# Two output tiles of batch 0 by seven half-size products, earlier loads, and VectorE's work in pairs of pairs

## The chip, the cores and the metric

The kernel runs on one core of a Trainium2 chip. A core has TensorE (PE in the profile; its weight loads are listed as PEld), VectorE (DVE), ScalarE (ACT), GpSimd (POOL) and SyncE (SP), each with its own instruction stream, and 16 DMA engines that all queues share. The engines run side by side and wait for one another through semaphores. The metric is the device time of one execution in microseconds (us), as the median of several runs.

## The reference

Two stages, in float32. The first is a block-sparse attention for 4 batches, 8 heads, 768 tokens and a head dimension of 64. Each query sees the 31 keys nearest to it and 24 block summaries (the maximum of 32 keys, the mean of 32 values); both share one softmax:

```python
k_sum = k.reshape(B, H, nb, block, D).max(axis=3)
v_sum = v.reshape(B, H, nb, block, D).mean(axis=3)
scores_l = scale * np.matmul(q, k.transpose(0, 1, 3, 2))      # masked to |i - j| < 16
scores_s = scale * np.einsum('bhsd,bhnd->bhsn', q, k_sum) + np.log(block)
a = softmax(np.concatenate([scores_l_masked, scores_s], axis=-1))
attn = np.matmul(a, np.concatenate([v, v_sum], axis=2))
```

The second is a feed-forward layer on the 3072 rows of 512 that come out of it (2048 hidden units):

```python
h = x @ w_in
g = h * (1.0 / (1.0 + np.exp(-1.702 * h)))
out = g @ w_out
```

## The kernel before, in words

Tokens are columns for most of the way. A batch has 768 tokens, split into two halves of 384 (`half` 0 and 1), each three tiles of 128. Heads go in four pairs (`p`), and two pairs make a group (`g`).

For each batch, the attention is: `scores` (small matmuls of keys with queries, then ScalarE's exponential into `a_sb`), `mask` (VectorE multiplies by `mk`), `values` (matmuls with the value rows `vw`, then VectorE's `norm`: a reciprocal and a multiplication for each pair, into `x2`), and a transposition into `xTT`: `tx` does it on TensorE with a copy by VectorE, `dx` by a DMA transpose of SP's queue. Keys stand in `kxs[s]` with three kinds of rows: their own, 16-column halos (`key_halos`) and the block maxima (`key_rows`); `rest_k` makes the maxima by a reduction and then the copies, for one pair. For batch 1 keys and queries are turned by TensorE (`tk`, `tq`), and there `rest_k` has its copies done by GpSimd; for batches 2 and 3 by DMA transposes (`xk`, `xq`). `value_rows` copies the values' halos by DMA, sums blocks of values on TensorE (`vsum`), adds them on VectorE (`block_sums`, into `vpart` and `vs`) and spreads the sums by two more DMAs (`sum_dmas`).

The feed-forward layer has a first matrix (`ff_in`, `ff_one`, `ff_open`: four matmuls of 384 columns for each of the 16 hidden tiles, then a gelu on ScalarE into `gTb`) and a second one in two forms. `ff_out` is the plain one: for an output tile of 128 tokens sixteen matmuls of 512 columns into one PSUM bank, in four parts. `product` is the other: the 2 x 2 blocks of two token tiles, hidden halves and output halves are multiplied with seven block products instead of eight, each of eight matmuls of 256 columns. That needs sums of weight blocks (`w_sum`, into `ws`) and of gelu tiles (`g_sums`, into `gs`), both on VectorE, and additions of the results on the way out (`keep_it`, `give`). The left tile of such a pair is tile t of half 0, the right one tile t of half 1.

Order: instructions stand on each engine's queue in the order of the program (`_Ordered`), so the order is written by hand. Batch 0's attention and half 0 come first (to line 1089). Then half 1 of batch 0 runs its first matrix (lines 1095 to 1099) with the `todo` list beside it: batch 1's turned keys and queries, and the sums of the weights. Its three output tiles follow, all plain (lines 1102 to 1108), with batch 1's attention beside them step by step (`plan1`, called by `beside`). The loop from line 1112 then takes batches 1 and 2: first matrix, then the three pairs of tiles by seven products in the order `seq`, with the next batch's attention beside them (`plan`). Batch 3 is done apart, with products in both matrices.

Loads: q, k and v come through GpSimd's queue, which also converts them (`load_turned`, `load_v`). A batch's loads are issued by `load_batch`: keys, values and queries. Two tiny GpSimd copies (`gate2`) hold the queue until certain transposes have landed, since they read what those write: lines 244 and 247 ahead of batch 3's keys and values, line 1133 ahead of batch 3's queries. At most eight loads of this queue are in flight; the next one waits for the one eight places before it.

PSUM banks for results come from two pools, `pmm` (tag `mm`, four banks) and `psb` (tag `big`, two double banks); a new tile waits until the readers of the bank's last contents are done.

Of the kernel before, what the change touches and what calls it, by code (L numbers as in the profile page):

```python
# [9 lines left out]
F32 = mybir.dt.float32  # L10
# [25 lines left out]
def kernel(  # L36
# [205 lines left out]
    def load_batch(b):  # L242
        if b == 3:
            pool.tensor_copy(out=gate2, in_=qTs[0][:, 0, 0:1])
        load_turned(k, b, kb2, "kb")
        if b == 3:
            pool.tensor_copy(out=gate2, in_=qTs[0][:, NP - 1, 0:1])
        if b == 1:
            load_turned(q, b, qb2, "qb", (0,))
        load_v(b)  # L250
        if b < 3:
            load_turned(q, b, qb2, "qb", (1,) if b == 1 else (0, 1))
# [89 lines left out]
    def flat_kx(p, s):  # L342
        return kx[p][s].rearrange("p t c -> p (t c)")

# [228 lines left out]

    def rest_k(p, s, eng=dve):
        ks = attp.tile([128, nb], BF16, name="ks", tag="ks")
        dve.tensor_reduce(out=ks.rearrange("p (j e n) -> p j e n", e=2, n=2),
                          in_=at(flat_kx(p, s), 0, [[256, NJ], [192, 2], [block, 2], [1, block]]),
                          axis=AX.X, op=ALU.max)
        key_halos(p, s, eng)
        key_rows(p, s, ks, eng)  # L580
# [16 lines left out]
    def values(b, half, g):  # L597
# [81 lines left out]
    def g_sums(j, eng=dve, which=(0, 1, 2, 3)):  # L679

        a1, a2 = gTb[:, j], gTb[:, j + NT // 2]
        l, r = slice(0, HALF), slice(HALF, S)
        for w in which:
            a, b_, op = {0: (a1[:, r], a2[:, r], ALU.add), 1: (gs[:, 0, j], a1[:, l], ALU.subtract),
                         2: (a1[:, l], a1[:, r], ALU.subtract), 3: (a2[:, l], gs[:, 1, j], ALU.subtract)}[w]
            eng.tensor_tensor(out=gs[:, w, j], in0=a, in1=b_, op=op)
# [84 lines left out]
    def product(b, t, what):  # L771
        n = NT // 2
        l = slice(t * 128, t * 128 + 128)
        r = slice(HALF + t * 128, HALF + t * 128 + 128)
        lo, hi = slice(0, N1), slice(N1, d_model)
        raw_l, raw_r = gTb[:, :, l], gTb[:, :, r]
# [41 lines left out]
        if what == 1:  # L818
            keep_it("s1")
        elif what == 2:  # L820
            give("o1", lo, "s1")
        elif what == 6:
            keep_it("s2")
        elif what == 5:
            keep_it("s5")
        elif what == 7:
            give("o2", hi, "s5")
            if last:
                store("o2", HALF + t * 128, hi)
        elif what == 3:  # L830
            give("o1", hi, "s2")
            store("o1", t * 128)
        else:
            give("o2", lo, None)
            store("o2", HALF + t * 128, lo if last else slice(0, d_model))
# [37 lines left out]
    gate2 = consts.tile([128, 1], BF16, name="gate2")  # L873
# [137 lines left out]
    for p in range(NP):  # L1011
# [5 lines left out]
    load_batch(1)  # L1017
# [6 lines left out]
             9: ["x00", "x01", "v10"], 10: ["v11"], 11: ["x10"]}  # L1024
# [59 lines left out]
    for i, (ms, part) in enumerate((ms, part) for part in range(4) for ms in range(JH)):  # L1084
        ff_out(0, ms, part)
        beside0(i)
        if i in (10, 11):
# [4 lines left out]
            6: [lambda: w_sum(2, 1)], 7: [lambda: w_sum(3, 0)], 8: [lambda: tk(2, 1, act)],   # L1092
            10: [lambda: w_sum(3, 1)], 9: [lambda: tq(0, 1, dve)], 11: [lambda: tk(3, 1, act)], 12: [lambda: tq(1, 1, dve)],
            15: [lambda: value_rows(1)]}
    ff_in(1, range(3))
    for nt in range(3, NT):
        ff_in(1, (nt,))
        for f in todo.get(nt, ()):
            f()
    exp_soon()  # L1100
    beside(1, -1)
    for i, (ms, part) in enumerate((ms, part) for ms in range(JH) for part in range(4)):
        ff_out(1, ms, part)
        beside(1, i)
        if i == 2:
            load_batch(2)
        if i in (9, 11):
            xk(i // 2 - 4, 0)
# [3 lines left out]
    for b in range(1, B - 1):  # L1112
# [5 lines left out]
        for n in range(0, NT, 2):  # L1118
            if n == 0:
                ff_open(order2[0:4], (lambda: tx(1, 1)) if b == 1 else None)  # L1120
            elif n == 2:
                for nt in order2[0:4]:
                    ff_one(1, nt)
                g_sums(0)
                g_sums(1)
            else:
# [3 lines left out]
                g_sums(n // 2, dve, (0, 1) if n + 2 == NT else (0, 1, 2, 3))  # L1130
# [15 lines left out]
        for t, what in seq:  # L1146
# [97 lines left out]
```

## Time and profile before

| what | value |
|---|---|
| median of three runs | 206.86 us (206.62 to 208.16) |
| the profiled execution | 206.51 us, of which 204.8 us is the span from the first to the last instruction |
| TensorE clock granted | 0.998 of full speed |
| instructions | 5857, of them 2364 matmuls |
| busy: TensorE, VectorE, ScalarE, GpSimd | 198.1, 140.4, 124.6, 92.7 us |
| HBM read, written | 27.26 MB, 6.29 MB |

Busy time is a mean over stages with different limits. The stages of this kernel in the span, by TensorE's chain: batch 0's attention to about 20 us; its first half's layer and second half's attention to 45; its second half's first matrix to 58; its second half's output with batch 1's attention to 75; batch 1's layer with batch 2's attention to 119.5; batch 2's layer with batch 3's attention to 163.5; batch 3's layer to the end. The profile's rows name what an instruction writes and reads, `out<-in`; a row of a group has the count, the sum of busy time, the mean of one in ns, the idle time of the engine before it and what ended that. In the timeline the first two numbers are start and duration in us.

### The profile page before, as it was taken

To read this page: it belongs to the slowest core of one execution; us is meant where nothing else is said; L and a number is where in the kernel's file an instruction comes from. 1 tells how busy PE (TensorE), PEld (TensorE's weight loads), DVE (VectorE), ACT (ScalarE), POOL (GpSimd) and SP (SyncE) were. 2 spreads that over 40 slices of the span, in tenths; PEclk is the share of its full clock that TensorE was granted. 3 is DMA by queue.
4 is the path that set the end of the run, shared out by engine and by line. 5 is a ranking of instruction groups with operands and counts; after the bars stand their busy time and mean duration, and the time that the engine had idled before them with its cause. 6 is when DMAs were issued, how large, how long until landed. Compare 5 with 4: busy or idle time off the path is not lost.

```text
span 204.8 us, 5857 instructions
## 1 busy us (share of the span) xinstructions
PE 198.1 (97%) x2364; PEld 137.4 (67%) x2364; DVE 140.4 (69%) x388; ACT 124.6 (61%) x238; POOL 92.7 (45%) x144
## 2 busy tenths in 40 slices
PE   6989999999999999999999999999999999999992
PEld 6667654556754566665888975657888865578881
DVE  6767894594856874897768689896759546658211
ACT  4385876638786717777871546778661467983220
POOL 7965389555999584002965035000000019990000
PEclk9999999999999999999999999999999999999999
DMA  5999999999999999999999989996023730000222
GB/s 117 153 159 202 207 211 213 195 156 232 134 143 151 177 176 168 159 175 132 123 196 127 154 151 142 122 261 137 0 106 90 160 111 3 0 0 3 102 102 104
DMA packets 95851, 27.93 MB, mean 136 GB/s; under 512 B 83649, under 2 KB 92881, under 8 KB 95825
## 3 DMA queue, kind: packets, MB, share of 16 engines
q0 software_dynamic: 69920, 13.44, 85.2%
q1 hardware_dynamic: 25904, 14.13, 33.2%
q8 instruction: 18, 0.29, 0.6%
q14 instruction: 9, 0.07, 0.1%
HBM read 27.26 MB, written 6.29 MB: 164 GB/s over the span
## 4 chain that ended last, share of the span: by engine, by line
PE 90%; DMA 4%; POOL 2%; DVE 1%; issue 1%; ACT 0%; POOLq 0%; DVEq 0%
PE ph L28 33%; PE poA L28 16%; PE po L28 11%; PE poB L28 7%; PE ps_av L28 4%; DMA v0n<-in_v_dram 4%; PE poC L28 4%; PE phA L28 4%; PE ps_s L28 3%; PE ps_t L28 1%; PE ps_x L28 1%; POOL kb L28 1%; PE phB L28 1%; PE phC L28 1%; PE phE L28 1%; PE ps_vs L28 1%
## 5 line engine op out<-in xcount | busy, mean ns | idle before, releaser
L28 PE MATMUL ph<-xT,w_in_sb 128*128 128x384 f16 x416 | 70.2, 326 | 0.1
L28 PEld LDWEIGHTS <-w_in_sb 128*128 128x128 f16 x452 | 43.7, 98 | 27.8 <-issue 0.2
L28 ACT ACTIVATE gT<-ph 128x384 f16<-128x384 f32 x104 | 49.9, 492 | 18.5 <-PE ph L28 18.1
L28 PEld LDWEIGHTS <-gT 128*128 128x128 f16 x312 | 28.8, 98 | 11.3 <-issue 0.2
L28 ACT ACTIVATE a_sb<-ps_s 128x768 bf16<-128x768 f32 (+1 forms) x32 | 25.0, 826 | 12.5 <-PE ps_s L28 12.5
L28 POOL DMA_DIRECT2D vw<-in_v_dram x36 | 24.6, 700 | 12.4 <-DMA kb<-in_k_dram 4.8
L28 PEld LDWEIGHTS <-gs 128*128 128x128 f16 x288 | 27.7, 98 | 3.4
L28 POOL TENSOR_TENSOR gs<-gT 128x384 f16<-128x384 f16 x9 | 8.2, 911 | 42.3 <-ACT gT L28 42.3
L28 PE MATMUL po<-w_out_sb,gT 128*128 128x512 f16 x96 | 23.6, 380 | 0.0
L28 DVE TENSOR_TENSOR a_sb<-a_sb,mk 128x768 bf16<-128x768 bf16 x28 | 14.9, 554 | 6.5 <-ACT a_sb L28 5.9
L28 PE MATMUL poA<-ws,gs 128*128 128x256 f16 x144 | 18.7, 273 | 0.0
L28 DVE TENSOR_TENSOR x<-ps_av,rc 128x384 f16<-128x384 f32 x32 | 17.8, 558 | 1.1
L28 DVE TENSOR_TENSOR gs<-gT 128x384 f16<-128x384 f16 (+1 forms) x34 | 13.4, 394 | 7.2 <-ACT gT L28 6.9
L28 POOL DMA_DIRECT2D qb<-in_q_dram x16 | 15.1, 956 | 1.8 <-DMA w_in_sb<-in_moe_w_in_dram 1.1
L28 POOL DMA_DIRECT2D kb<-in_k_dram x15 | 14.5, 976 | 0.9 <-POOLq L1228 0.8
L28 PEld LDWEIGHTS <-kx 64*128 64x128 bf16 (+1 forms) x372 | 9.4, 95 | 6.8 <-issue 4.4
L28 DVE TENSOR_REDUCE ks<-kx 128x24 bf16<-128x768 bf16 x12 | 11.4, 949 | 3.4 <-ACT kx L28 3.2
L28 ACT ACT_TABLE_LOAD x10 | 12.8, 1283 | 1.0 <-PEq L1228 0.8
L28 ACT ACTIVATE osb<-poA 128x256 f32<-128x256 f32 x9 | 3.5, 384 | 16.0 <-PE poA L28 16.0
L28 ACT ACTIVATE s<-poA 128x256 f32<-128x256 f32 x11 | 4.2, 386 | 11.2 <-PE poA L28 11.2
L28 PEld LDWEIGHTS <-a_sb 128*64 128x64 bf16 (+2 forms) x400 | 7.8, 108 | 2.8 <-issue 1.3
L28 PE MATMUL poA<-ws,gT 128*128 128x256 f16 x72 | 9.3, 273 | 0.0
(117 smaller groups left out, 282.7 us busy)
## 6 DMA issues: line engine op xcount, KB each, us to landing
out_dram<-osb SPq DMA_DIRECT2D x23, 256.0 KB, 3.3
kb<-in_k_dram POOLq DMA_DIRECT2D x15, 192.0 KB, 7.1
qb<-in_q_dram POOLq DMA_DIRECT2D x12, 192.0 KB, 10.9
vw<-in_v_dram POOLq DMA_DIRECT2D x36, 64.0 KB, 5.7
w_out_sb<-in_moe_w_out_dram POOLq DMA_DIRECT2D x4, 512.0 KB, 13.0
w_in_sb<-in_moe_w_in_dram POOLq DMA_DIRECT2D x3, 512.0 KB, 12.9
vw<-vs SPq DMA_DIRECT2D x6, 198.0 KB, 6.1
v0n<-in_v_dram POOLq DMA_DIRECT2D x4, 192.0 KB, 8.1
```

Source lines behind the costliest of these rows:

```text
L28: r = f(*a, **kw)
```

## The change

Four things change together.

1. Batch 0's second half: tile 0 (tile 3 of the batch) stays plain, tiles 1 and 2 are the left and right tile of one set of seven products. `product` takes the pair of tiles as an argument, and `g_sums_tiles` makes the sums for these two tiles alone, for two pairs of hidden tiles at once. The first matrix of this half runs its hidden tiles in the order j, j + 8 (`order2`) so that the sums can start early. The stretch has eleven steps where it had twelve, and `x10` moves up beside `v11`.
2. Batch 1's key rows: `rest_k` leaves `tk`, and with it GpSimd; `rest_k2` makes two pairs at once on VectorE, at steps 7 and 13 of the first matrix. Batches 2 and 3 use it too, two calls in place of four.
3. `g_sums` takes two hidden pairs at once where it can (n=2), and `values` norms both pairs of a group by one reciprocal and one multiplication for batches 2 and 3.
4. `load_batch` and the gates are gone. Batch 2's values are asked for ahead of batch 0's second first matrix, its keys at steps 7 and 12 of it, its queries at the third output step; batch 3's keys and queries during batch 1's first matrix, its values after batch 1's first product. The DMA transposes of keys move up to steps 4 and 7 of the output stage before, those of queries to the start of the next first matrix.

```diff
@@ new functions
+    def rest_k2(g, s):
+        flat = kxs[s].rearrange("p i t c -> p (i t c)")
+        o, n = 2 * g * NQ * 128, 2 * NJ
+        ks = attp.tile([128, 2, nb], BF16, name="ks", tag="ks")
+        dve.tensor_reduce(out=ks.rearrange("p i (j e n) -> p (i j) e n", e=2, n=2),
+                          in_=at(flat, o, [[256, n], [192, 2], [block, 2], [1, block]]),
+                          axis=AX.X, op=ALU.max)
+        dve.tensor_copy(out=at(flat, o + 256 + 96, [[256 * NJ, 2], [256, NJ - 1], [1, 16]]),
+                        in_=at(flat, o + 256 - 16, [[256 * NJ, 2], [256, NJ - 1], [1, 16]]))
...
+        for i in range(2):
+            key_rows(2 * g + i, s, ks[:, i])
+    def g_sums_tiles(j, L, R, eng):
+        js, js2 = slice(j, j + 2), slice(j + NT // 2, j + NT // 2 + 2)
+        l, r = slice(L * 128, L * 128 + 128), slice(R * 128, R * 128 + 128)
+        o = [gs[:, w, js, 0:128] for w in range(4)]
+        for w, (a, b_, op) in enumerate(((gTb[:, js, r], gTb[:, js2, r], ALU.add), (o[0], gTb[:, js, l], ALU.subtract),
+                                         (gTb[:, js, l], gTb[:, js, r], ALU.subtract),
+                                         (gTb[:, js2, l], o[1], ALU.subtract))):
+            eng.tensor_tensor(out=o[w], in0=a, in1=b_, op=op)
@@ tk
-        rest_k(p, s, pool)
@@ values
+        if b > 1:
+            pv = ps.rearrange("p (i c) -> p i c", i=2)[:, :, 0:390].rearrange("p i (n c) -> p i n c", c=D + 1)
+            rc = attp.tile([128, 2, 2 * JH, 1], F32, name="rc2", tag="rc2")
+            dve.reciprocal(out=rc, in_=pv[..., D:D + 1])
+            dve.tensor_mul(x2[g].rearrange("p h j i d -> p i (h j) d"), pv[..., 0:D],
+                           rc.to_broadcast([128, 2, 2 * JH, D]))
+            return
@@ plan1
-             9: ["x00", "x01", "v10"], 10: ["v11"], 11: ["x10"]}
+             9: ["x00", "x01", "v10"], 10: ["v11", "x10"]}
@@ batch 0, second half
-    ff_in(1, range(3))
-    for nt in range(3, NT):
-        ff_in(1, (nt,))
-        for f in todo.get(nt, ()):
+    load_v(2)
+    ff_in(1, order2[0:3])
+    for i in range(3, NT):
+        ff_in(1, (order2[i],))
+        for f in todo.get(i, ()):
             f()
+        if i in (6, 10, 14):
+            g_sums_tiles((i - 6) // 2, JH + 1, JH + 2, dve)
     exp_soon()
     beside(1, -1)
-    for i, (ms, part) in enumerate((ms, part) for ms in range(JH) for part in range(4)):
-        ff_out(1, ms, part)
+    steps1 = [("seven", what) for what in (1, 2, 5, 6, 7, 3, 4)] + [("plain", part) for part in range(4)]
+    for i, (kind, what) in enumerate(steps1):
+        if kind == "plain":
+            ff_out(1, 0, what)
+        else:
+            product(0, 1, what, (JH + 1, JH + 2))
+        if i == 0:
+            g_sums_tiles(6, JH + 1, JH + 2, dve)
         beside(1, i)
         if i == 2:
-            load_batch(2)
-        if i in (9, 11):
-            xk(i // 2 - 4, 0)
+            load_q(2, 0, 1)
+        if i in (4, 7):
+            xk(i // 3 - 1, 0)
@@ batches 1 and 2
-                g_sums(0)
-                g_sums(1)
+                g_sums(0, n=2)
...
-                if n == 0 and b > 1:
-                    pool.tensor_copy(out=gate2, in_=xTT[1][1][:, 1, 0:1])
-                    load_turned(q, b + 1, qb2, "qb")
+                if n == 0:
+                    xq(0, s)
+                    xq(1, s)
+                    if b == 1:
+                        load_k(3, 0, 1)
                 if n // 2 == 1:
                     value_rows(s)
-                if n // 2 == 2 * b:
-                    xq(0, s)
-                    xq(1, s)
-                if n // 2 in (2, 3, 4, 5):
-                    rest_k(n // 2 - 2, s)
+                if n // 2 == 2 and b == 1:
+                    load_q(3, 0, 1)
+                if n // 2 in (2, 4):
+                    rest_k2(n // 4 - 1, s)
...
                 if i == 1:
-                    load_batch(b + 2)
-                if i in (16, 18):
-                    xk(i // 2 - 8, b % 2)
+                    load_v(b + 2)
+                if i in (4, 7):
+                    xk(i // 3 - 1, b % 2)
```

More of the change, by code (lines that the diff above doesn't have):

```diff
@@ L240, in clear_sums, with load_k, load_q @@
             eng.memset(v6[g * 32:g * 32 + nb, :, g, D:D + 1], float(block))
[L242 to L252, printed above, removed]
+    def load_k(b, *gs_):
+        load_turned(k, b, kb2, "kb", gs_)
+    def load_q(b, *gs_):
+        load_turned(q, b, qb2, "qb", gs_)
     def load_w_in(n0, n1):
@@ L572, in xq @@
                      in_=qb2[g].rearrange("p i a h d -> p (i a h d)"), transpose=True)
[L574 to L580, printed above, removed]
     a_sb, x_sb, x2 = {}, {}, {}
@@ L768, in ff_gelu, with product @@
         gelu("CBAE".index(bank) % 2, j + (NT // 2 if bank in "AE" else 0), ff_now[j, bank])
-    def product(b, t, what):
+    def product(b, t, what, tiles=None):
         n = NT // 2
-        l = slice(t * 128, t * 128 + 128)
-        r = slice(HALF + t * 128, HALF + t * 128 + 128)
+        L, R = tiles or (t, JH + t)
+        l = slice(0, 128) if tiles else slice(t * 128, t * 128 + 128)
+        ll, r = slice(L * 128, L * 128 + 128), slice(R * 128, R * 128 + 128)
         lo, hi = slice(0, N1), slice(N1, d_model)
-        raw_l, raw_r = gTb[:, :, l], gTb[:, :, r]
+        raw_l, raw_r = gTb[:, :, ll], gTb[:, :, r]
         w1, w2 = w_out_sb[:, 0:n], w_out_sb[:, n:]
@@ L1016 @@
     clear_values(dve, 1)
-    load_batch(1)
+    load_k(1, 0, 1)
+    load_q(1, 0)
+    load_v(1)
+    load_q(1, 1)
     plan0 = {1: ["q0", "q1", "q2"], 2: ["q3", "s0", "s1"], 4: ["s2", "s3"], 6: ["v0", "v1"], 8: ["x0"], 9: ["x1"]}
```

34 lines of the change are left out of this document (22 added, 12 removed).

## The prediction

> **What bounds the kernel now.** I read the page first, then the chain of waits, then the windows, and last the timeline and the groups of the one stretch that the change rebuilds. The page:
>
> ```profile
> PE 198.1 (97%) x2364; PEld 137.4 (67%) x2364; DVE 140.4 (69%) x388; ACT 124.6 (61%) x238; POOL 92.7 (45%) x144
> ...
> PE 90%; DMA 4%; POOL 2%; DVE 1%; issue 1%; ACT 0%; POOLq 0%; DVEq 0%
> ```
>
> TensorE is the bound: busy for 97% of the span, and 90% of the chain that ended last. So a change gains only what it takes from TensorE's own stream, and loses by whatever makes that stream wait. How dense the stream is stands in the chain of waits (start, duration, what):
>
> ```profile
> 81.27 15.71 PE ph L28 x96
> 96.98 0.46 PE ps_s L28 x24
> 97.43 0.98 PE poA L28 x8
> 98.41 0.87 PE poB L28 x8
> ...
> 119.54 5.20 PE ph L28 x32
> ```
>
> 96 matmuls of 384 columns take 15.71 us, 0.164 each; eight of 256 take 0.87, 0.109 each. The first eight after a change of tile shape take 0.98, so a switch costs 0.11. These paces follow the column count and each piece begins where the last one ended. In the stages of batches 2 and 3 there is thus no hole that earlier loads, earlier transposes or shorter VectorE work could fill: what the change does there can only lose, if something becomes late. The change touches the stream itself in one stretch, the last three output tiles of batch 0:
>
> ```profile
> 58.63 1.83 PE po L28 x8
> 60.47 0.34 PE ps_t L28 x6
> ...
> 62.00 0.28 PE ps_s L28 x12
> ...
> 67.00 0.50 PE ps_av L28 x24
> ...
> 71.93 0.50 PE ps_av L28 x24
> 72.43 0.97 PE po L28 x4
> 73.40 0.50 PE ps_av L28 x24
> ```
>
> Here too no hole is left. Eight matmuls of 512 columns take 1.83 - 0.11 = 1.72 us, 0.216 each (0.215 to 0.217). What the other engines do meanwhile is in the windows (sum, then PE, PEld, DVE, ACT and POOL busy):
>
> ```profile
> 49.00:58.10 9.10, 9.10 (x121) 6.14 (x119) 7.14 (x10) 7.55 (x16) 7.99 (x18) 1.00 1.92 173
> 58.10:75.20 17.10, 17.10 (x281) 9.56 (x272) 12.73 (x33) 10.48 (x16) 14.00 (x23) 1.00 1.71 161
> ```
>
> VectorE has 2.0 us free in the first of them, just where the change gives it more to do.
>
> **The change, part by part.**
>
> *Seven products.* Two tiles of sixteen 512-column matmuls, 32 x 0.216 = 6.91 us, become 56 matmuls of 256 columns, 56 x 0.109 = 6.10. TensorE gains 0.8 us; the number of shape switches stays about the same. A rule of the Trainium skill speaks against this: "TensorE: Matmul & The Clock Gate", section "Back-to-back issue gap", gives about 131 ns a matmul for 512 columns and 81 for 128 where weight loads and matmuls alternate. By it the 32 would cost 4.2 us and the 56 at least 4.5, an estimate from that page, so that the products would lose 0.3. The rows above, with 0.216 and 0.109, contradict it.
>
> *VectorE before the products.* The half-size products need sums of gelu tiles: sixteen instructions of 2 x 128 columns, twelve of them before the stage begins, where VectorE had none. Batch 1's key rows move from GpSimd to VectorE, for two pairs at once. Durations, by form:
>
> ```profile
> L28 DVE TENSOR_TENSOR gs<-gT 128x384 f16<-128x384 f16 x33 | 12.1, 365 | 7.2 <-ACT gT L28 6.9
> L28 DVE TENSOR_REDUCE ks<-kx 128x24 bf16<-128x768 bf16 x12 | 11.4, 949 | 3.4 <-ACT kx L28 3.2
> ...
> L28 DVE COPY kx<-kx 128x80 bf16<-128x80 bf16 x16 | 2.1, 173 | 0.0
> ...
> L28 DVE TENSOR_TENSOR gs<-gT,gs 128x2304 f16<-128x2304 f16 x1 | 1.4, 1353 | 0.0
> ```
>
> From 384 to 2304 elements a sum grows by 988 ns: 0.515 ns an element over a fixed 167. One of 256 elements then takes 0.30 us, and a set of four, where two wait for the one before, about 1.0. A reduction of 1536 elements takes 949 + (949 - 167) = 1.73 us; it can't be under 0.95 (one old one) nor over 1.90 (two), and I take 1.73 since the elements are twice as many. The five copies behind it, 0.17 us and a little more each, overlap to about 0.7. The events between which this must fit:
>
> ```profile
> 55.20 0.50 PE L28 MATMUL ps_t<-wide,qb 128*128 128x128 bf16 x6
> ...
> 58.23 0.29 DVE L28 COPY vpart<-ps_vs 128x128 f32<-128x128 f32 x1 [1.18 <-PE ps_vs L28]
> ...
> 58.56 1.18 DVE L28 TENSOR_TENSOR vs<-ps_vs,vpart 32x128 bf16<-32x128 f32 x4
> ...
> 59.60 1.49 ACT L28 ACTIVATE a_sb<-ps_s 128x768 bf16<-128x768 f32 x2
> ...
> 73.48 0.56 DVE L28 TENSOR_TENSOR x<-ps_av,rc 128x384 f16<-128x384 f32 x1
> ```
>
> VectorE's order becomes: second query copy (its transposes end at 55.70), reduction, copies, four sums, the block sums of the values (`vpart`, `vs`), the last four sums, the first addition into an output tile, the third query copy. From 55.74 on, 0.47 + 1.65 + 0.7 + 1.0 (durations less their overlap) lead to 59.55, where `vpart` now starts at 58.23: 1.3 late. `vs` ends at 59.55 + 0.33 + 1.18 = 61.05.
>
> *What waits for it.* After the scores (58.63) TensorE has product 1, 0.98, product 2, 0.87, and transposes, 0.34: product 5 is due at 60.82. It opens a bank that the block sums read, free at 61.10: a wait of 0.28, and it ends at 61.97. The next transposes take a bank that is free only after the last four sums (to 62.0) and the addition:
>
> ```profile
> L28 PE MATMUL poA<-ws,gs 128*128 128x256 f16 x144 | 18.7, 273 | 0.0
> ...
> L28 ACT ACTIVATE s<-poA 128x256 f32<-128x256 f32 x11 | 4.2, 386 | 11.2 <-PE poA L28 11.2
> ...
> L28 DVE TENSOR_TENSOR osb<-poA,s 128x256 f32<-128x256 f32 x9 | 3.8, 423 | 4.0 <-PE poA L28 4.0
> ```
>
> ScalarE's copy of product 1 stands behind the two exponentials (to 61.09) and ends at 61.5, so VectorE decides: 62.0 + 0.42, a wait of 0.48. The scores of pair 2 wait 0.12 for the query copy behind that addition. Product 7 follows product 6 in the same bank with only twelve score matmuls (0.28) and a switch between; product 6 drains for 0.16 (273 ns for a pace of 109) and its copy out takes 0.39, with some 0.1 for the two signals, so product 7 waits 0.25 (in later batches another product stands there). At the stretch's end `x10` moves up beside `v11`. The last norm of `v10` ends at 74.04, 2.11 after `v10` began; TensorE now needs only 0.50 + 0.97 + 0.50 = 1.97 to get there and then loads weights, which I put at 0.2: a wait of 0.34.
>
> Waits: 0.28 + 0.48 + 0.12 + 0.25 + 0.34 = 1.47 us, all in the stream that sets the end. With VectorE's new instructions at 0.8 of my times the first wait goes and the second, which then hangs on ScalarE's copy, stays: net 0.4 slower. At 1.2 of them VectorE is 1.0 later: net 1.6.
>
> *VectorE in batches 2 and 3.* Sums and norms of two pairs save a fixed 0.17 us each, behind TensorE: 0, with no hole to fill and no wait added.
>
> *Loads.* GpSimd loses its copies and its gates. Batch 2's values are asked for right behind batch 1's last query load, ahead of the keys, and the queue then runs on through keys, queries and all of batch 3 where a gate held it:
>
> ```profile
> 53.45 2.04 POOL L28 DMA_DIRECT2D qb<-in_q_dram  x2
> ...
> 95.86 0.41 POOL L28 COPY gate<-qT 128x1 bf16<-128x1 bf16 x1 [16.73 <-DMA qT<-qb]
> ```
>
> So from 55.5 us to beyond 110 loads are always in flight. Two transfers of SP's queue are near a deadline. Of the block sums (`vw<-vs`), of batch 2's `x`, and of keys beside query loads (76 to 82 us), the rows are:
>
> ```profile
> L28 SPq DMA_DIRECT2D vw<-vs x2: 585/593/601, 59.8 to 60.4; - x2
> ...
> DMA to landing us min/median/max: 3.0/4.3/5.6
> ```
>
> ```profile
> 116.60 2.59 SPq L28 DMA_TRANSPOSE xT<-x  x2
> ```
>
> ```profile
> xT<-x SPq DMA_TRANSPOSE x4, 2.8
> ```
>
> ```profile
> kx<-kb SPq DMA_TRANSPOSE x2, 9.7
> ```
>
> The second block-sum copy lands by 60.4 + 5.6 = 66.0 and `v00` reads it at 67.0. It will go out 1.3 later, and `v00` is 1.2 later, so 0.9 us of slack stay, with loads beside the whole flight. The last `x` transpose goes out at about 117.9 and lands at 120.7; TensorE reads it at 119.54 + 16 x 0.164 = 122.2. Both cost 0 while they land as now. The far ends are the 9.7 us that a transpose took beside query loads: 9.7 - 5.6 - 0.9 = 3.2 us for the sums, 9.7 - 2.8 - 1.5 = 5.4 for `x`. I take 0, the sums' own row being nearest, and since the queue, two gates earlier, should run empty near 117 us.
>
> Sum: -0.8 + 1.47 = +0.67. The profiled execution took 206.51 us (204.8 of span and 1.7 around it), so 207.2; the median, 206.86, lies 0.35 above that execution, so on it **207.5 us**.
>
> **The rivals.**
>
> *A. The products pay.* VectorE keeps up and nearly no wait is left: net -0.8 to 0.1, 206.1 to 207.0. For it: the 2.0 us that VectorE has free from 49 to 58.1. Against it: the waits of product 7 and `x10`, 0.59 together, don't come from the backlog.
>
> *B. The load queue that never rests makes SP's transfers late,* the other side. Place: the block sums before `v00`, or the `x` transposes before batch 2's first stage. It decides from 0.9 us (sums) or 1.5 us (`x`) of later landing on. Price: 0.5 to 5.4 us beside the 0.67, 208.0 to 212.9, most likely near 209.5. For it: 9.7 against 2.8. Against it: less is left to load by 117 us.
>
> *C. VectorE's new shapes are slow* (strided halves, patterns of four steps), over 1.2 of my times: net 1.6 to 2.5, 208.5 to 209.4.
>
> *D. Paired spacing.* A matmul's pace depends on its weight load more than on its columns, the products lose 0.3 and the waits come on top: 208.6. The rows speak against it. The Trainium skill's page named above has this rule.
>
> **How the numbers follow.** Forecast (net 0.1 to 1.5: 207.0 to 208.4) 0.51; A 0.15; B 0.23; C 0.10; D 0.01. About 1% is what a measurement of this kernel can tell from no change, so the edges are 204.8 and 208.9. Faster than that needs 2 us where TensorE's stream gives 0.8: 0.03. Slower: most of B, 0.17, and some of C and D, 0.06: 0.23. Within: 0.74. The range takes in nearly all of A and all but the far end of B, 206.2 to 209.9; what lies outside has under 2 in 10.
>
> **What would show it.** In the profile of the changed kernel: `poA`, `poB`, `poC` with 0.87 for eight between 58 and 68 us; between 60 and 66 us waits of TensorE for VectorE of a few tenths each; one for `x` near 75; VectorE without idle time from 55.7 to 64; 81 to 160 us again without holes. I am wrong if those waits are missing (A), if holes stand before `v00` or near 120 us with a DMA as their releaser (B), or if the reduction takes over 1.9 us or a sum over 0.36 (C).

## The result, and the profile after

The changed kernel takes 215.95 us (median of four runs, 215.31 to 218.51), the kernel before 206.79 in the same comparison: a ratio of 1.045, 95% interval 1.035 to 1.055. It is slower by 9 us, outside the predicted range of 206.2 to 209.9. The profiled execution took 216.49 us with a span of 214.5. Medians in this document are of all executions, while ratios leave out the few slow ones, so the two can differ by some tenths of a us.

The page of the kernel after, its first line and the shares of the chain that ended last:

```profile
PE 199.8 (93%) x2388; PEld 140.5 (66%) x2388; DVE 140.8 (66%) x359; ACT 124.9 (58%) x240; POOL 87.1 (41%) x125
...
PE 68%; DMA 20%; DVE 6%; POOL 2%; issue 1%; ACT 0%; SPq 0%; POOLq 0%; DVEq 0%
```

TensorE's busy time hardly moved (198.1 to 199.8 us). On the chain it fell from 90% to 68%, and DMA rose from 4% to 20%: the kernel now waits for transfers. Where, the chain of waits shows (start, duration, what). First two rows of the kernel before that the prediction did not show:

```profile
30.53 1.73 PE po L28 x8
...
125.27 15.71 PE ph L28 x96
```

The same chain of the kernel after:

```profile
31.12 1.73 PE po L28 x8
...
62.55 7.78 DMA vw<-vs
...
84.26 15.71 PE ph L28 x96
...
108.70 15.64 DMA vw<-in_v_dram
...
124.88 10.45 DMA vw<-in_v_dram
...
135.62 15.71 PE ph L28 x96
```

The first piece of the plain output starts 0.6 us later in this execution (31.12 against 30.53), before anything that was changed. From there to the 96 matmuls behind batch 2's block sums it takes 53.1 us instead of 50.7, 2.4 more, with a copy of the block sums (`vw<-vs`) on the chain. From these to the 96 behind batch 3's it takes 51.36 instead of 44.00, 7.4 more, with loads of batch 3's values on the chain. The rest of the span is 0.6 shorter. So there are two holes, and both end with a DMA.

The timeline of TensorE shows what ended each wait (start, duration, what, and in brackets the idle time before it and its releaser):

```profile
61.94 1.03 PE L28 MATMUL poB<-ws,gs 128*128 128x256 f16 x8 [0.53 <-DVE vs L28]
63.45 0.50 PE L28 MATMUL ps_t<-wide,qb 128*128 128x128 bf16 x6 [0.47 <-DVE osb L28]
...
70.47 0.54 PE L28 MATMUL ps_av<-vw,a_sb 128*64 128x65 bf16 x23 [1.05 <-DMA vw<-vs]
...
77.60 0.51 PE L28 MATMUL ps_x<-ident,x 128*128 128x128 f16 x6 [0.20 <-DVE x L28]
```

```profile
124.03 1.55 PE L28 MATMUL poA<-ws,gT 128*128 128x256 f16 x8 [2.37 <-DVE osb L28]
125.37 4.29 PE L28 MATMUL ph<-xT,w_in_sb 128*128 128x384 f16 x18
130.19 2.44 PE L28 MATMUL ph<-xT,w_in_sb 128*128 128x384 f16 x14 [0.53 <-DMA xT<-x]
132.56 0.54 PE L28 MATMUL ps_vs<-vw,E 64*32 64x128 bf16 x40
134.04 0.21 PE L28 MATMUL ps_vs<-vw,E 64*32 64x128 bf16 x1 [0.95 <-DMA vw<-in_v_dram]
135.37 0.25 PE L28 MATMUL ps_vs<-vw,E 64*32 64x128 bf16 x7 [1.12 <-DMA vw<-in_v_dram]
```

The largest wait of the first hole is that of `v00` for the block sums, 1.05 of the 2.4 us. The second is four waits: for `osb`, for `x`, and twice for batch 3's values. VectorE's own timeline takes the first of them one step further back:

```profile
123.55 0.42 DVE L28 TENSOR_TENSOR osb<-poA,s 128x256 f32<-128x256 f32 x1 [3.12 <-DMA out_dram<-osb]
```

VectorE could not write an output tile, since the last store out of that buffer had not landed. All of these are transfers of SP's queue, or loads of GpSimd's. The landing times by group (count, size, median us from issue to landing), of the kernel before around 110 to 119 us:

```profile
out_dram<-osb SPq DMA_DIRECT2D x2, 256.0 KB, 3.2
```

and of the kernel after, around 61.5 to 63 us (the first row) and 113 to 122 us (the others):

```profile
vw<-vs SPq DMA_DIRECT2D x2, 198.0 KB, 7.4
...
out_dram<-osb SPq DMA_DIRECT2D x2, 256.0 KB, 8.0
...
xT<-x SPq DMA_TRANSPOSE x4, 9.0
```

Block sums took 4.3 us before and 7.4 now, stores 3.2 and 8.0, `x` transposes 2.8 and 9.0. What differs is GpSimd's loads. In the kernel before batch 2's begin at 59.76, just as the block sums go out, and batch 3's values are all issued by 110.5; now loads are in flight beside each of these transfers.

The four waits in the second hole add up to 4.97 us, not 7.4. Part of the rest is in the windows. The first number, which the prediction's caption calls the sum, is the length of the window; then come the busy times of PE, PEld, DVE, ACT and POOL with the number of instructions, the granted clock, the DMA share and GB/s:

```profile
122.00:124.00 2.00, 0.00 (x0) 0.00 (x0) 0.45 (x2) 0.00 (x0) 0.38 (x1) 1.00 1.21 175
124.00:126.00 2.00, 1.97 (x10) 1.30 (x10) 1.97 (x3) 0.38 (x1) 0.98 (x2) 0.60 1.45 229
126.00:128.00 2.00, 2.00 (x8) 1.00 (x7) 2.00 (x3) 0.00 (x0) 0.00 (x0) 0.55 1.60 159
128.00:130.00 2.00, 1.66 (x11) 0.88 (x9) 0.97 (x1) 1.60 (x4) 0.00 (x0) 1.00 1.60 194
```

Behind the wait of 2.4 us TensorE's granted clock is about half for some 4 us. The last product of the stage needs 1.34 us (124.03 to 125.37) where eight matmuls take 0.87, and the first 18 matmuls of the next stage 4.29 where 18 x 0.164 = 2.95: 1.8 us more. With the waits that is 6.8 of the 7.4. The rest is in how the brackets count: they give idle time only, and leave out the 0.1 to 0.2 us for which the matmul ahead of a wait runs out. From start to start of the same rows all of it is there: 2.5 us more ahead of the last product, 0.5 in it, 1.9 in the 32 matmuls of the next stage, 2.5 in the block sums.

### The profile page after: what moved, and what is told of

Same layout as the page of the kernel before. It is cut to its first block, busy times and chain, and to the rows that moved or that the text cites. A ratio compares the mean times of both kernels' runs of the same rounds, so it can differ in the third digit from the quotient of the medians.

```text
span 214.5 us, 5865 instructions
## 1 busy us (share of the span) xinstructions
PE 199.8 (93%) x2388; PEld 140.5 (66%) x2388; DVE 140.8 (66%) x359; ACT 124.9 (58%) x240; POOL 87.1 (41%) x125
## 4 chain that ended last, share of the span: by engine, by line
PE 68%; DMA 20%; DVE 6%; POOL 2%; issue 1%; ACT 0%; SPq 0%; POOLq 0%; DVEq 0%
PE ph L28 28%; PE poA L28 12%; DMA vw<-in_v_dram 12%; PE poB L28 6%; PE po L28 5%; DMA v0n<-in_v_dram 4%; DMA vw<-vs 4%; PE phA L28 4%; PE poC L28 3%; PE ps_av L28 3%; PE ps_s L28 2%; DVE x L28 2%; POOL kb L28 1%; PE ps_x L28 1%; PE ps_t L28 1%
## 5 line engine op out<-in xcount | busy, mean ns | idle before, releaser
L28 PE MATMUL ph<-xT,w_in_sb 128*128 128x384 f16 x416 | 71.7, 330 | 0.6 <-DMA xT<-x 0.5
L28 PEld LDWEIGHTS <-gs 128*128 128x128 f16 x320 | 30.6, 98 | 4.5 <-issue 0.6
L28 DVE TENSOR_TENSOR gs<-gT 128x768 f16<-128x768 f16 (+3 forms) x30 | 13.8, 460 | 16.0 <-ACT gT L28 16.0
L28 PE MATMUL poA<-ws,gs 128*128 128x256 f16 x160 | 20.8, 273 | 0.1
L28 DVE TENSOR_TENSOR x<-ps_av,rc 128x384 f16<-128x384 f32 (+1 forms) x24 | 16.6, 690 | 0.8
L28 PE MATMUL po<-w_out_sb,gT 128*128 128x512 f16 x64 | 15.5, 380 | 0.0
L28 PE MATMUL poA<-ws,gT 128*128 128x256 f16 x80 | 10.9, 282 | 2.4 <-DVE osb L28 2.4
L28 ACT ACTIVATE s<-poA 128x256 f32<-128x256 f32 x13 | 5.0, 385 | 11.4 <-PE poA L28 11.4
L28 DVE TENSOR_REDUCE ks<-kx 128x48 bf16<-128x1536 bf16 x6 | 10.5, 1748 | 0.8 <-ACT kx L28 0.7
L28 PE MATMUL poB<-ws,gs 128*128 128x256 f16 x80 | 10.4, 273 | 0.5 <-DVE vs L28 0.5
## 6 DMA issues: line engine op xcount, KB each, us to landing
w_out_sb<-in_moe_w_out_dram POOLq DMA_DIRECT2D x4, 512.0 KB, 12.9
```

Source lines behind the costliest of these rows:

```text
L28: r = f(*a, **kw)
```

## The experiments

**Theory L**: the loads. GpSimd's load queue, without its holds, is in flight beside SP's transfers, which land too late; and batch 3's values stand last in that queue. **Rival P**: the seven products and VectorE's backlog push the work around them, and the loads are only where it shows.

To compare the profiles independently of how late the first 30 us were in each execution, this table gives three stretches of each, from TensorE's timeline: A from the first `po` to the matmuls behind batch 2's block sums, B from there to those behind batch 3's, C from there to the end of the span.

| kernel | A | B | C | median us | before us | ratio (95%) |
|---|---|---|---|---|---|---|
| before | 50.84 | 44.00 | 79.60 | | | |
| after | 53.24 | 51.36 | 78.95 | 215.95 | 206.79 | 1.045 (1.035 to 1.055) |
| loads_back | 53.94 | 44.01 | 78.98 | 210.81 | 207.24 | 1.019 (1.013 to 1.025) |
| loads_back_held | 53.73 | 45.68 | 79.00 | 210.83 | 207.24 | 1.015 (1.009 to 1.021) |
| plain_new_loads | 52.29 | 50.08 | 78.98 | 214.09 | 207.24 | 1.032 (1.029 to 1.036) |
| v3_before_q3 | 51.98 | 48.65 | 78.94 | 213.41 | 207.24 | 1.028 (1.025 to 1.031) |
| q3_gated | 51.77 | 44.00 | 79.00 | 208.93 | 207.47 | 1.005 (1.002 to 1.009) |
| before_no_gates | 50.99 | 48.00 | 79.00 | 210.52 | 207.47 | 1.015 (1.010 to 1.020) |
| pool_rows | 52.63 | 44.00 | 78.98 | 208.59 | 207.47 | 1.006 (1.002 to 1.009) |
| pool_rows_v2 | 52.10 | 45.95 | 78.93 | 210.45 | 207.47 | 1.014 (1.009 to 1.019) |
| products_alone | 52.81 | 44.00 | 79.44 | 210.05 | 207.65 | 1.010 (1.006 to 1.013) |
| late_sums | 51.44 | 44.00 | 78.97 | 207.73 | 207.65 | 1.002 (0.998 to 1.005) |

### The old loads under the new work

```diff
@@ loads_back, against after: load_batch and its copies into gate2 as in the kernel before
-    load_v(2)
     ff_in(1, order2[0:3])
...
-            load_q(2, 0, 1)
-        if i in (4, 7):
-            xk(i // 3 - 1, 0)
+            load_batch(2)
+        if i in (8, 10):
+            xk(i // 2 - 4, 0)
...
-                if n == 0:
-                    xq(0, s)
-                    xq(1, s)
-                    if b == 1:
-                        load_k(3, 0, 1)
+                if n == 0 and b > 1:
+                    pool.tensor_copy(out=gate2, in_=xTT[1][1][:, 1, 0:1])
+                    load_turned(q, b + 1, qb2, "qb")
...
-                    load_v(b + 2)
-                if i in (4, 7):
-                    xk(i // 3 - 1, b % 2)
+                    load_batch(b + 2)
+                if i in (16, 18):
+                    xk(i // 2 - 8, b % 2)
@@ loads_back_held, against loads_back
+            pool.tensor_copy(out=gate2[0:32], in_=vs[0:32, H - 1, 0:1])
             load_batch(2)
```

> The changed kernel with part 4 alone undone (loads issued, held by the copies into gate2 and transposes placed as before; keys' transposes at output steps 8 and 10). Theory L (the load queue that never rests makes SP's transfers and batch 3's values late, and is nearly all of the +9.2 us): the hole before batch 2's block sums goes entirely, the products' waits stay, 207.2 us; but GpSimd has no key copies any more that held batch 2's loads to 59.8 us, so these start at once behind batch 1's, the block-sum copies may still land 6 to 8 us after issue, and v00 then waits up to 2 us more: 207.0 to 209.5. Rival P (the products and VectorE's backlog are the cause, and the loads only follow): 213 to 216.

> The same, and batch 2's loads held by one more tiny GpSimd copy that reads vs, so that they start when the block sums are made (about 61.6 us). Theory L: no wait of TensorE for vw<-vs and none near 120 us; what is left are the products' saving of 0.8 and their waits of 1.3 to 1.5: 207.0 to 207.6, within 1% of before. Rival P: 213 to 216. If it stays 1 us or more above 207.5, part 3 or the order of hidden tiles costs something that I have not seen.

With part 4 undone the second hole is gone entirely (B is 44.01), so 7.4 of the 9 us are part 4's. But 210.81 is above both of L's figures, and the first hole is even larger. The landing of the block sums, in loads_back:

```profile
vw<-vs SPq DMA_DIRECT2D x2, 198.0 KB, 8.0
```

and in loads_back_held:

```profile
vw<-vs SPq DMA_DIRECT2D x2, 198.0 KB, 3.4
```

In the kernel before, GpSimd made batch 1's key copies between the loads of batches 1 and 2, and these held the queue back for 4 us. Its timeline there, first and last:

```profile
55.53 0.75 POOL L28 COPY kx<-kx 128x80 bf16<-128x80 bf16 x3
...
59.39 0.43 POOL L28 COPY kx<-ks 128x288 bf16<-128x288 bf16 x1
59.76 4.05 POOL L28 DMA_DIRECT2D kb<-in_k_dram  x4
```

Part 2 took them away, so restoring the program order of the loads does not restore the hold. With an explicit one the sums land in 3.4 us, and no wait for `vw<-vs` is left. The time is the same nevertheless, for another reason, in TensorE's timeline and the chain of loads_back_held:

```profile
84.24 0.25 PE L28 MATMUL ps_vs<-vw,E 64*32 64x128 bf16 x7 [0.92 <-DMA vw<-in_v_dram]
```

```profile
84.49 17.39 PE ph L28 x96
```

Batch 2's loads started 2.1 us later than in the kernel before (61.9 against 59.8; 0.3 of it is this execution's later start), its last values land at 84.2, and the block sums need them at about 82. Two waits, 0.74 and 0.92, were followed by 17.39 us for matmuls that take 15.71. The windows of loads_back_held behind them, with the granted clock before the last two numbers:

```profile
86.00:87.00 1.00, 1.00 (x5) 0.50 (x4) 0.97 (x2) 0.49 (x1) 0.00 (x0) 0.50 3.51 137
87.00:88.00 1.00, 1.00 (x5) 0.48 (x4) 1.00 (x4) 0.25 (x1) 0.00 (x0) 0.50 2.76 147
```

So both my figures missed; the hold moves the loss to the next deadline.

### Plain tiles with the new loads, and the order of batch 3's loads

```diff
@@ plain_new_loads, against after: no g_sums_tiles, hidden tiles in order 0 to 15, x10 at step 11
-    steps1 = [("seven", what) for what in (1, 2, 5, 6, 7, 3, 4)] + [("plain", part) for part in range(4)]
+    for i, (ms, part) in enumerate((ms, part) for ms in range(JH) for part in range(4)):
+        ff_out(1, ms, part)
...
@@ v3_before_q3, against after
                 if n // 2 == 2 and b == 1:
-                    load_q(3, 0, 1)
+                    load_v(3)
...
-                    load_v(b + 2)
+                    load_q(3, 0, 1)
```

> The changed kernel with its three tiles of batch 0's second half plain again (no sums of gelu tiles there, x10 at its own step) and the new loads, key rows on VectorE and merged sums kept. Theory L: the second hole stays whole (7.4), the first shrinks by the backlog that is gone (VectorE 0.4 to 1.0 us earlier): 213.5 to 215.5. Rival P: 206.5 to 208.

> The changed kernel with batch 3's values asked for ahead of its queries, places exchanged, nothing else. If the order in the queue is what makes the second hole (values last in line): values land by about 118 us, and 7 of the 7.4 us go: 208.5 to 209.5. If it is that loads of any kind are in flight beside SP's output stores and x transposes: only the waits for the values (0.95 + 1.12 us in the profile) go, the wait for osb (2.4) and for x (0.5 and what precedes it) stay: 213 to 214.5.

Without a single product the kernel still takes 214.09 us. Rival P, 206.5 to 208, is out for the second hole. TensorE's timeline of plain_new_loads has the same one:

```profile
124.18 1.03 PE L28 MATMUL poA<-ws,gT 128*128 128x256 f16 x8 [2.89 <-DVE osb L28]
...
129.10 0.50 PE L28 MATMUL ph<-xT,w_in_sb 128*128 128x384 f16 x2 [1.29 <-DMA xT<-x]
130.72 2.44 PE L28 MATMUL ph<-xT,w_in_sb 128*128 128x384 f16 x14 [1.11 <-DMA xT<-x]
```

The first hole is there too, if smaller: `v00` waits 0.20 and 0.39 us for the block sums.

With the values ahead of the queries no wait for values is left, and 213.41 us come out: what was forecast if loads of any kind beside SP's transfers are the cause. The waits for the output stores and for `x` stay; the transposes in v3_before_q3:

```profile
xT<-x SPq DMA_TRANSPOSE x4, 9.3
```

So the values' place in the queue is a smaller part of the second hole (B falls by 2.7), the loads beside SP's transfers the larger.

### The hold alone, on and off

```diff
@@ q3_gated, against after
                 if n == 0:
-                    xq(0, s)
-                    xq(1, s)
+                    if b == 2:
+                        pool.tensor_copy(out=gate2, in_=xTT[1][1][:, 1, 0:1])
+                        load_q(3, 0, 1)
+                    else:
+                        xq(0, s)
+                        xq(1, s)
...
-                    load_q(3, 0, 1)
+                    load_v(3)
+                if n // 2 == 4 and b == 2:
+                    xq(0, s)
+                    xq(1, s)
...
-                if i == 1:
-                    load_v(b + 2)
@@ before_no_gates, against before: the three copies into gate2 taken out
-            pool.tensor_copy(out=gate2, in_=qTs[0][:, 0, 0:1])
-            pool.tensor_copy(out=gate2, in_=qTs[0][:, NP - 1, 0:1])
-                    pool.tensor_copy(out=gate2, in_=xTT[1][1][:, 1, 0:1])
```

> The changed kernel with batch 3's values ahead of its queries, and the queries (loads and transposes) put back behind the copy that waits for the last x transpose, as before; batch 2's loads as changed. If the second hole comes from loads in flight beside SP's x transposes and output stores, it goes but for what the values, now landing near 118 us, still overlap: TensorE waits 0 to 2 us between 118 and 136 us, and 208.5 to 210.5 us come out (the first hole, 2.3, and the products' 0.5 stay). If it were the transposes of keys at their new places that make x late, 213 again.

> The kernel before without its three tiny GpSimd copies that hold batch 3's loads; the order keys, values, queries and all places stay. If the gates do what theory L says, x transposes land 5 us or more after issue beside the queries' loads, and TensorE waits 1 to 4 us before batch 2's first matrix: 208 to 211. If the gates are idle decoration and only the place of the values in the queue counts: 206.5 to 207.5.

With the values first, a hold on the four query loads, with their transposes behind it, brings B back to 44.00 and the time to 208.93. The keys' transposes are still at their new places, so these alone were not the cause. The `x` transposes of q3_gated, with the values still in flight beside the first of them:

```profile
xT<-x SPq DMA_TRANSPOSE x4, 5.2
```

That is early enough; in the prediction's working they had 1.5 us to spare on 2.8, here 5.2 median does no harm.

One term of the expectation missed: the first hole did not stay. As far as stretch A goes, the kernel after, v3_before_q3 and q3_gated have the same program, and yet A is 53.24, 51.98 and 51.77, since `v00` waits in the first of these profiles alone. The block sums landed 7.4, 6.2 and 4.7 us after issue there (medians of two). So the 1.05 us at `v00` is what one execution had, not a fixed cost, and what A has without it, 0.9 to 1.1 us over the kernel before, is the products with their waits.

The other way round, the kernel before without its three tiny copies loses 3 us (1.015), as theory L said, though in another place. Its query transposes of batch 2 (issued from 84 to 100 us), and TensorE's wait for them:

```profile
qT<-qb SPq DMA_TRANSPOSE x2, 11.2
```

```profile
104.17 0.52 PE L28 MATMUL ps_s<-qT,kx 64*128 64x64 bf16 x24 [2.16 <-DMA qT<-qb]
```

They took 5.6 in the kernel before, where the hold kept batch 3's loads out until they had landed. Two more waits, 1.31 us ahead of that stage's first scores (released by VectorE's sums) and 0.23 for `osb`, make up most of the rest of the 4.0 in B; for the `x` transposes, where the expectation looked, no wait is listed. This is the cleanest pair: nothing differs but the holds.

### The products without the loads

```diff
@@ products_alone: part 1 on the kernel before (g_sums_tiles, product with tiles, steps1, order2, x10 beside v11)
@@ pool_rows, against loads_back
-    def rest_k2(g, s):
+    def rest_k2(g, s, eng=dve):
...
-            7: [lambda: w_sum(3, 0), lambda: rest_k2(0, 1)],
+            7: [lambda: w_sum(3, 0), lambda: rest_k2(0, 1, pool)],
...
-            12: [lambda: tq(1, 1, dve)], 13: [lambda: rest_k2(1, 1)],
+            12: [lambda: tq(1, 1, dve)], 13: [lambda: rest_k2(1, 1, pool)],
...
-             9: ["x00", "x01", "v10"], 10: ["v11", "x10"]}
+             9: ["x00", "x01", "v10"], 10: ["v11"]}
...
-                ff_open(order2[0:4], (lambda: tx(1, 1)) if b == 1 else None)
+                ff_open(order2[0:4], (lambda: (tx(1, 0), tx(1, 1))) if b == 1 else None)
@@ pool_rows_v2, against pool_rows: values of batch 2 ahead of its keys in load_batch, and its key rows one place later
-        if i in (8, 10):
-            xk(i // 2 - 4, 0)
...
                     value_rows(s)
+                    if b == 1:
+                        xk(0, 0)
+                        xk(1, 0)
@@ late_sums, against pool_rows
-        if i in (6, 10, 14):
+        if i in (6, 10):
             g_sums_tiles((i - 6) // 2, JH + 1, JH + 2, dve)
     exp_soon()
+    g_sums_tiles(4, JH + 1, JH + 2, dve, 4, (0, 1))
...
-        if i == 0:
-            g_sums_tiles(6, JH + 1, JH + 2, dve)
         beside(1, i)
+        if i == 2:
+            g_sums_tiles(4, JH + 1, JH + 2, dve, 4, (2, 3))
```

> The kernel before with part 1 alone: seven products for two tiles, sums of gelu tiles, order of hidden tiles, x10 beside v11; key rows, loads and gates as before (keys' transposes at steps 8 and 10 of eleven). Theory L: the saving of 0.8 and the waits (vs, osb, product 7, x10), 0.6 to 1.3: the stretch from the first matrix of batch 0's second half to that of batch 1 takes 29.8 to 30.5 us where it took 29.96, and the time is 0.0 to 0.5 above before. Rival P: 2 us or more above.

> The changed kernel with the loads as before, the key rows' copies of batch 1 back on GpSimd (VectorE keeps the two reductions), where they hold batch 2's loads to about 60 us again, and x10 made together with x11. Theory L: block sums go out at 60.4 to 61 us and land in 3 to 5; the wait for vs (0.2 to 0.5) goes, the one for osb (0.47) shrinks, the last one (0.20) goes; batch 2's values, which had 0.9 us to spare before, decide: 206.0 to 207.2, and up to 1 more if they come late.

> The same with batch 2's values ahead of its keys, and the keys' transposes behind the halo copies of the next stage. The values land near 72 us and can't be late; keys land at about 82 and their transposes near 92, where the reductions stand now: 206.0 to 206.8. If transposes beside the query loads take 10 us again, VectorE waits for kx, but TensorE does not until the scores at 97.

> The kernel with key rows' copies on GpSimd and the loads as before, and the last half of the gelu tiles' sums taken out of the way: two of them behind the block sums, for four pairs at once, two behind the third query copy. If the waits for vs and osb are VectorE's order and nothing else, both go (0.65 of the stretch), the block sums leave 1 us earlier and v00 doesn't wait: the stretch takes 29.4 to 29.9 us, and the time is 0.1 to 0.5 below before. If a wait of 0.3 or more stays in that place, ScalarE's copy of product 1 behind the two exponentials sets it.

Part 1 alone costs 2.0 us by the ratio (1.010; 2.4 by the medians), not 0 to 0.5, with every load and hold as before. That is the figure set for rival P: for the first hole it is half right. TensorE's timeline of products_alone:

```profile
59.26 0.59 PE L28 MATMUL ps_vs<-vw,E 64*32 64x128 bf16 x47 [0.68 <-DVE qT L28]
...
70.23 0.54 PE L28 MATMUL ps_av<-vw,a_sb 128*64 128x65 bf16 x23 [0.75 <-DMA vw<-vs]
```

The first row is a wait for VectorE's query copy, which now stands behind sums of gelu tiles. With these sums the block sums go out 2.1 us later (61.9 against 59.8; 0.8 of it is this execution's later start), into batch 2's loads, which start at 61.2 here, ahead of them; the second copy lands 7.6 us after its issue instead of 5.6. So the first hole has two parents: VectorE makes the sums late, and the loads make their copies slow. pool_rows, at 208.59, has the same wait (0.65), the one for `osb` has not shrunk (0.48), and the time is above its 206.0 to 207.2.

pool_rows_v2 (210.45, for 206.0 to 206.8 expected) removes that wait and finds another: the keys' transposes go out only at 87.1 us, behind the block sums of the next stage, VectorE waits for them, and two products wait for VectorE (0.92 and 0.56 near 101 us), which I had excluded. It also shows VectorE's work slower beside GpSimd's. GpSimd's timeline, then VectorE's, of pool_rows_v2:

```profile
57.11 1.10 POOL L28 COPY kx<-kx 128x160 bf16<-128x160 bf16 x3
58.16 0.91 POOL L28 COPY kx<-ks 128x288 bf16<-128x288 bf16 x2
```

```profile
58.27 0.50 DVE L28 TENSOR_TENSOR gs<-gT 128x256 f16<-128x256 f16 x1
...
61.18 0.28 DVE L28 TENSOR_TENSOR gs<-gT 128x256 f16<-128x256 f16 x1
```

The same sum takes 0.50 us beside GpSimd's copies and 0.28 without them.

late_sums is the best version with products: 207.73 against 207.65, a ratio of 1.002 (0.998 to 1.005), no difference that can be told. I had expected 0.1 to 0.5 us of gain. Its waits for `vs` and for the block sums are gone; of the one for `osb` 0.18 is left, 0.35 from start to start. VectorE's row behind it names the reason:

```profile
62.42 0.42 DVE L28 TENSOR_TENSOR osb<-poC,s 128x256 f32<-128x256 f32 x1 [0.74 <-ACT s L28]
```

That is ScalarE's copy of product 1 behind two exponentials, the case that the expectation named. With the gap at product 7 (0.21) and two waits at the next first matrix (0.19 and 0.20) the small waits use up more than the saving: from start to start they add 1.4 us to the stream, and A is 0.6 longer than before. No version that I ran beats the kernel before.

## Why the prediction was wrong, point by point

**TensorE is the bound: right, and its consequence.** It was said that in the later stages a change can only lose if something becomes late. That is what happened, at two places, and rival B had named both.

**"I take 0, the sums' own row being nearest, and since the queue, two gates earlier, should run empty near 117 us": the step that failed.** It holds 8.4 of the 9.2 us in this profile (1.05 at `v00`, which the products share in, and 7.4). The queue did not run empty near 117, a figure for which the prediction gives no working; its last load landed at 135.3 us (124.88 + 10.45). Two things made it late. The first is in GpSimd's timeline of the kernel after, at the first keys of batch 3:

```profile
85.39 2.02 POOL L28 DMA_DIRECT2D kb<-in_k_dram  x2 [10.73 <-DMA kx<-kb]
```

The gate is gone, but these loads overwrite what batch 2's key transposes read, and so wait for them; "from 55.5 us to beyond 110 loads are always in flight" was wrong. The second is the landing time of the values' loads, between 96 and 112 us in the kernel before and then after:

```profile
vw<-in_v_dram POOLq DMA_DIRECT2D x12, 64.0 KB, 4.7
```

```profile
vw<-in_v_dram POOLq DMA_DIRECT2D x6, 64.0 KB, 16.5
```

Not only SP's transfers are slow beside the loads, the loads are slow beside them; in before_no_gates, where nothing but the holds is gone, the values' loads take 12.9 as well. And each load waits for the one eight places before: the last went out at 124.88, when the one issued at 108.70 had landed (108.70 + 15.64). The bound for the sums was sound (up to 3.2; measured 1.05), and the sums landed 7.4 us after issue against 4.3. The bound for `x` was 5.4 us at 9.7; the transposes took 9.0, but TensorE waited only 0.53 for them, since the wait for `osb` and its slow matmuls came first. What no bound of mine held is that the same contention also delays the output stores (2.37 us of wait), that batch 3's values, last in the queue, have a deadline of their own (2.07), and that a wait of TensorE is followed by slow matmuls (1.8). I had looked at two of SP's transfers that were near a deadline, not at all that share the engines.

**Rival B was the right mechanism with too small a price and chance**: 0.5 to 5.4 us, for one place or the other, and 0.23, where it was 1.05 at `v00` and 7.4 later, most of it by stores and values that B did not name. The argument against it ("less is left to load by 117 us") was the failed step again. The row for it, 9.7 against 2.8, was in the prediction, and it was the case to be expected while loads are in flight.

**Rule and row.** On arbitration the Trainium skill's "DMA: Bandwidth & Descriptors", section "Queues, rings and completion order", says that each DMA engine takes packets in turn from the queue rows that have work. The traces agree: SP's transfers do not stop beside the loads, they land two to three times as late (2.8 to 9.0, 3.2 to 8.0).

**Seven products save 0.8 us: right within 0.1.** In TensorE's timeline the output pieces of the stretch, from start to start and without the waits, take 10.2 to 10.3 us in late_sums where they take 11.0 in the kernel before: 0.7 to 0.8. (The spread is product 5, whose end a wait hides.) Rival D is refuted, and with it the 131 ns of the page that the prediction weighed (the Trainium skill, "TensorE: Matmul & The Clock Gate", section "Back-to-back issue gap"): eight matmuls of 256 columns take 0.87 us here as well, 0.109 each.

**The waits: right in kind, the sum somewhat small.** Predicted and measured, in the kernel after: product 5 for `vs` 0.28 and 0.53; `osb` 0.48 and 0.47; the gap at the scores of pair 2 0.12 and 0.13; at product 7 0.25 and 0.12; at `x10` 0.34 and 0.20. By these brackets the sum is 1.45 for 1.47. From start to start against the kernel before, which is what the stream pays, it is 2.0: product 5 comes 0.68 later, the transposes behind it 0.64, the pieces before and at product 7 0.14 and 0.13, `x10` 0.26 and what follows 0.1; the gap at the scores of pair 2 is hardly new, since the kernel before takes 0.44 from the same transposes to these scores and this one 0.47. So with 0.67 predicted for products and waits together, q3_gated, which has neither hole, shows 0.93 in A. No run shows the 0.2 that was put on a weight load ahead of `x10`: TensorE starts 0.04 after the norm. The reduction came out as worked out, and so did the sums, by VectorE's groups of the kernel after:

```profile
L28 DVE TENSOR_REDUCE ks<-kx 128x48 bf16<-128x1536 bf16 x6 | 10.5, 1748 | 0.8 <-ACT kx L28 0.7
...
L28 DVE TENSOR_TENSOR gs<-gT 128x256 f16<-128x256 f16 x8 | 2.3, 284 | 0.7 <-ACT gT L28 0.7
```

1.75 for 1.73, and 0.28 for 0.30. Mis-sized were the five copies of the key rows: 1.0 us on the chain for 0.7, which fits the wait for `vs`, 0.25 larger than predicted; in q3_gated they take 0.84 and the wait is 0.30. Rivals A and C are out: the waits are there, and the new shapes are not slow.

**VectorE in batches 2 and 3 by pairs: 0, right as far as the stretches tell.** B is 44.00 before and 44.00 or 44.01 in every variant that has the merged sums and norms but neither late loads nor late keys. Part 3 was not run by itself.

**What stays open.** Stretch C is 0.6 shorter in most variants, also in before_no_gates, which changes nothing there but the holds. The traces put it in the last 6 us of one execution: to the start of the last product but one C takes 73.85 us in the kernel before and 73.84 in before_no_gates; then, in the kernel before, the last product starts 0.2 later, behind an addition of VectorE's that is 0.36 later, and the last stores land 0.4 later. So it is nothing that the change does. The first 30 us differ by up to 3.3 us between profiles of kernels whose program is the same up to there. The longest, q3_gated, lost them to a granted clock of 0.50 from 16 to 22 us (below); the kernel after is 0.6 later than before since batch 0's first values landed at 15.03 instead of 14.45. The others I did not follow up, and with one profile of each, how long `v00` waits in a typical execution stays open too.

## What to carry to other kernels

A copy that only holds a queue is part of the schedule: ask of each one what it keeps apart, and put its removal in as every transfer of the other queues at the contended landing time, stores included. When an instruction moves from one engine to another, look at what it held back where it stood; GpSimd's key copies were a hold that nobody had written as one. And in a stream without holes a saving of 0.7 us on the bounding engine is spent by four waits that the profile lists at 0.2 us each, so the engines that feed it must have that time free before the change, in order, not as a sum.

## What the hardware did that I had not expected

A wait of TensorE can cost twice its length or more. After a wait of 2.37 us the granted clock was 0.55 to 0.60 for 4 us, 1.8 us more (kernel after), and much the same behind one of 2.41 in v3_before_q3. After two waits of 0.74 and 0.92 within 2 us it was 0.50 from 86 to 88 us, and 96 matmuls took 17.39 us instead of 15.71 (loads_back_held). In q3_gated a wait of 1.56 us for batch 0's first values, to 14.99, was followed by 0.50 from 16 to 22 us. Waits of 2.89 us in plain_new_loads and 2.16 in before_no_gates had no such sequel: the granted clock was 1.00, and eight matmuls behind the first of them took their usual time. The Trainium skill, "TensorE: Matmul & The Clock Gate", section "What's actually happening", has half clock after an idle window of about 3.4 us and says that the windows run freely. The half clock agrees; that waits well under 3.4 us set it off in four profiles and not in two others fits windows of which a wait covers enough or not, which no run here shows directly.

VectorE's sum of 256 elements took 0.50 us instead of 0.28 while GpSimd copied, in pool_rows_v2.
